# The first part of the query weights as two loads of 64 partitions from two queues, in a decode kernel of attention and a mixing MLP

## The chip, the cores and the metric

The kernel runs on one core of a Trainium2 chip. The core has five engines with queues of their own: TensorE (PE, matrix products), VectorE (DVE), ScalarE (ACT), GpSimd (POOL) and SyncE (SP), and 16 DMA engines that move data between the chip's main memory and the core's SBUF of 128 partitions. In this kernel loads are issued by SyncE and, for one small one, by ScalarE. The metric is the device time of one execution in microseconds (us); lower is better.

## What is computed

One token passes through two layers. The first is attention with a cache of keys and values: 32 query heads, 8 key heads, 16,384 cached positions of 128 values each; the second is a layer norm, a small mixing block and an MLP of width 1792. With one token, the mixing block's shifts by one or two positions leave nothing but zeros, so only x itself passes through it.

```python
def _A_ref(x, k_cache, v_cache, wq, wo):
    q = (x @ wq).reshape(B, Sq, Hq, Dh).transpose(0, 2, 1, 3)
    k = jnp.repeat(k_cache, rep, axis=1)
    v = jnp.repeat(v_cache, rep, axis=1)
    scores = jnp.einsum("bhqd,bhkd->bhqk", q, k) * (Dh ** -0.5)
    p = _softmax(scores, axis=-1)
    o = jnp.einsum("bhqk,bhkd->bhqd", p, v)
    return o.transpose(0, 2, 1, 3).reshape(B, Sq, Hq * Dh) @ wo

h = x + _A_ref(_layernorm(x), k_cache, v_cache, wq, wo)
x1 = hn + hs        # hn = _layernorm(h); hs is zero for one token
return h + x1 + _gelu(_layernorm(x1) @ w3) @ w4
```

Everything is bf16. The two caches are 33.6 MB each, wq and wo 4.2 MB each, w3 and w4 1.8 MB each: 79.2 MB are read once.

## The kernel before

The 8 key heads are worked through in four pairs. For each pair 8.4 MB of keys go to the buffer kb (two halves of 128 x 32 KB) and 8.4 MB of values to vb (128 partitions of 64 KB). VectorE transposes the keys into kt (line 656), TensorE multiplies them with the query (line 667), a softmax follows on VectorE and ScalarE, and TensorE multiplies its result with the values (line 708). The buffer vb first holds the query weights wq (4 rows of wq, 32 KB, in each partition), and kb at the end holds wo, w3 and w4.

The program is written as a list of operations for each engine, with the tiles that each reads and writes; from these a small class derives the waits. Within an engine the order is the order of writing. All large loads are issued by SyncE through the helper load (line 474, the line that the profile shows for every load), in this order: the query weights in two loads, the keys of pair 0, the values of pair 0, and so on to wo, w3 and w4. A load waits only until its buffer has been read for the last time.

At the start (lines 586 to 590) ScalarE issues the load of x (1 KB, as 4 rows of 128 values), and SyncE the first WQ = 2048 columns of each partition's share of wq ("wq0", 4 KB a partition, 0.5 MB), then the other 28 KB a partition ("wq1", 3.5 MB), then the first keys. Meanwhile GpSimd makes an identity matrix and clears two tiles (lines 608 and 609), VectorE copies a corner of the identity to the tile quarter (line 601, which waits for x), TensorE spreads x over the partitions with it (line 603), and VectorE works out the layer norm's mean and root (lines 544 to 582) and some masks (lines 611 to 620). The tile xn (line 623) is the normed x. It waits for both weight loads, and the 32 products of line 632 that make the query wait for it. When these are done vb is free and SyncE issues the first values.

Of the kernel before, what the change touches and what calls it, by code (L numbers as in the profile page):

```python
# [356 lines left out]
NCH = D // 128  # L357
# [3 lines left out]
WQ = 2048  # L361
WO = ((0, 20), (20, 32))
VP = 1
# [22 lines left out]
def bass_sequential_preLN__gqa_block_cached__mixer_s_mlp__decode_kernel(  # L386
# [13 lines left out]
    with ExitStack() as ctx:  # L400
# [26 lines left out]
        st = [sb(f"st{i}", [128, 16], FP32) for i in range(2)]  # L427
        added = sb("added", [128, 2], FP32)
        sti = [sb(f"sti{i}", [128, 2, 2], I32) for i in range(2)]
        xn = sb("xn", [128, NCH], BF16)  # L430
# [23 lines left out]
        hT = sb("hT", [128, NCH, 32], FP32)  # L454
# [6 lines left out]
        wq_sb, wo_sb = vb, kb[0]  # L461
# [11 lines left out]
        def load(name, dst, src, key, by="SP", also=()):  # L473
            P.op(by, lambda e: e.dma_start(dst, src), w=[key, *also], dma=name)  # L474
# [54 lines left out]
        def piece(cuts, m):  # L529
            return [lo <= m < hi for lo, hi in cuts].index(True)  # L530
# [52 lines left out]
                r=[(S, 8), (T, 0)], w=[(S, 6 + n) for n in ns])  # L583


        load("x4", x4[:, :], A_x[0, 0:1, :].rearrange("o (q j) -> (o q) j", q=4), "x4", "ACT")
        wq_in = A_wq.rearrange("(p k) c -> p (k c)", k=NCH)
        load("wq0", wq_sb[:, 0:WQ], wq_in[:, 0:WQ], "wq0")
        load("wq1", wq_sb[:, WQ:NCH * HQ * DH], wq_in[:, WQ:NCH * HQ * DH], ("v", 0), also=[("v", x) for x in range(1, VP)])
        load_keys(0, 0)  # L590

# [1 line left out]
        for n in range(2):  # L593
# [8 lines left out]
            r=["ident_f", "x4"], w=["quarter"])  # L602
# [9 lines left out]
            r=["ident_f"], w=["row32"])  # L612
        dve(lambda e: e.tensor_reduce(maskdd[:, :], ident_f[:, :].rearrange("p (n d) -> p d n", d=4), AX.X, ALU.add),
            r=["ident_f"], w=["maskdd"])
# [3 lines left out]
        for z, src, key, of, n in ((zo, row32[:, :].rearrange("p (g n h) -> p g h n", g=2, h=REP), "zo", "row32", 4),  # L618
# [3 lines left out]
                src.unsqueeze(3).to_broadcast([128, 2, REP, 4, n]), AX.X, ALU.add), r=[of], w=[key])  # L622
        dve(lambda e: e.tensor_scalar(xn[:, :], hT[:, :, 0], st[0][:, 0:1], st[0][:, 6:7],  # L623
                                      ALU.add, ALU.mult),
            r=["hT", (("st", 0), 0), (("st", 0), 6), "wq0"] + [("v", x) for x in range(VP)], w=["xn"])

        keys = [("s", 0), ("s", 1), ("O", 0), ("O", 1), "A", "mn", "spare0", "spare1"]
        wq_k = wq_sb[:, 0:NCH * HQ * DH].rearrange("p (k c) -> p k c", k=NCH)
        for i, key in enumerate(keys):
            P.part("query", i)  # L630
            for k in range(NCH):
                pe(lambda e, k=k: e.matmul(row[:, bass.ds(P.b + P.b0, 512)], copies(xn[:, k:k + 1], 128),  # L632
                                           wq_k[:, k, bass.ds(P.c + P.c0, REP * DH)], start=(k == 0), stop=(k == NCH - 1)),
                   r=["xn"], also=[("v", x) for x in range(VP)], w=["n" if key == "mn" else key], bank=[key])
        P.part()
        for g in range(2):
            half = banks[64 * g:64 * g + 64, PAIRS * g:PAIRS * g + PAIRS, :].rearrange("p j c -> p (j c)")
            for b in range(2):
# [3 lines left out]
                    r=["n" if x == "mn" else x for x in keys[PAIRS * g:PAIRS * g + PAIRS]], w=["qcol"],  # L642
# [141 lines left out]
        for n, (lo, hi) in enumerate(W4):  # L784
# [4 lines left out]
            r=["o_m"], w=["o_f"])  # L789
        dve(lambda e: e.tensor_copy(o_b[:, :], o_f[:, :]), r=["o_f", ("r", 0, 0)], w=["o_b"])  # L790

        for r_ in range(32):
# [4 lines left out]
               r=["o_b"] + [("r", 0, n) for n in (piece(WO, r_),) if n], w=[("O", 0)], bank=[("O", 0)],  # L797
# [4 lines left out]
        for n in range(2):  # L802
            dve(lambda e, n=n: e.tensor_copy(osum[:, 256 * n:256 * n + 256], O_ps[0][:, 256 * n:256 * n + 256]),  # L803
                r=[("O", 0)], w=[("osum", n)], bank=[("O", 0)])
        for q in range(4):
            pe(lambda e, q=q: e.matmul(h_ps[32 * q:32 * q + 32, 0:128], copies(row32[:, 0:1], 32),
                                       osum[:, q * 128:(q + 1) * 128], start=True, stop=True),
               r=[("osum", q // 2), "row32"], w=[hkey], bank=[hkey])
# [4 lines left out]
            r=["hT", (S, 0)] + [("r", 1, 0)], w=["hc"])  # L813
# [3 lines left out]
        for k in range(NCH):  # L817
            for q in range(4):
                pe(lambda e, k=k, q=q: e.matmul(s_ps[32 * q:32 * q + 32, 0, 0:FQ], hc[:, k, :],
                                                w3_sb[:, k, q * FQ:(q + 1) * FQ], start=(k == 0), stop=(k == NCH - 1)),  # L820
                   r=["hc"] + [("r", 1, n) for n in (piece(W3, k),) if n], w=[("s", 0)], bank=[("s", 0)])
# [4 lines left out]
            r=["xs", (S, 6), "hr"], w=[hkey], bank=[hkey])  # L826
# [9 lines left out]
        for m in range(NHC):  # L836
# [5 lines left out]
            for o in range(4):  # L842
# [5 lines left out]
                   r=[("hcol", 2 * m // NHC)] + [("r", 1, len(W3) + n) for n in (piece(W4, m),) if n],  # L848
                   w=[hkey], bank=[hkey])
# [7 lines left out]
             r=[("fin", 0), ("fin", 1)], w=["out"], dma="out")  # L857
# [32 lines left out]
```

## Time and profile before

| | |
|---|---|
| runs timed, median (lowest to highest) | 189.47 us (189.44 to 189.67), 3 runs |
| profiled execution: span from the first to the last instruction | 188.3 us |
| mean clock granted to TensorE in it | 0.916 |
| busy: PE, DVE, ACT, POOL | 124.1, 115.8, 13.7, 4.6 us |
| read from main memory | 79.17 MB, 420 GB/s over the span |
| first issue of a load | 0.73 us |
| last load (w4) lands | 186.2 us |

The page gives the profiled execution's span and no other time of it. Its times count from the span's start. "L656" is line 656 of the kernel, "kt<-kb" is an operation that reads kb and writes kt, and "<-DMA" after a time says that a transfer ended the engine's wait. A name with q (SPq, ACTq) is an engine's instruction queue, where a load is issued; the transfer itself runs on the DMA engines behind it. q1 is the DMA queue of SyncE's loads, q10 that of ScalarE's.

### The profile page before, as it was taken

How to read it: one execution, taken by the hardware profiler on the slowest of the kernel's cores; microseconds unless marked ns; L12 is line 12 of the kernel's file. 1: busy time of each engine (PE TensorE's matmuls, PEld its weight loads, DVE VectorE, ACT ScalarE, POOL GpSimd, SP SyncE). 2: the span in 40 equal slices, each digit the busy share in tenths (PEclk: the TensorE clock that was granted, in tenths of full speed). 3: DMA queues.
4: the chain of work that ended last, by engine and by line, in shares of the span. 5: the costliest groups of instructions: out<-in, count | busy, mean ns of one | idle time of the engine just before them, and what ended most of it. 6: DMA issues, size and time to landing. Idle time of an engine off the chain costs nothing.

```text
span 188.3 us, 2375 instructions
## 1 busy us (share of the span) xinstructions
PE 124.1 (66%) x760; PEld 48.3 (26%) x761; DVE 115.8 (62%) x138; ACT 13.7 (7%) x21; POOL 4.6 (2%) x8
## 2 busy tenths in 40 slices
PE   0109700698979978897910019799799889775772
PEld 0104200233322522332500003333244333222221
DVE  5730741999636998936300069993699898633173
ACT  3000200000004000004000000000400000500012
POOL 8100000000000000000000000000000000000000
PEclk9999985569999999999995557999999999999999
DMA  7999999999799999987999999998999996999994
GB/s 252 445 418 445 445 445 446 445 445 445 334 445 446 445 557 418 418 390 334 446 445 445 445 446 445 445 445 334 445 446 445 543 390 292 445 432 411 433 429 193
DMA packets 2607, 79.19 MB, mean 421 GB/s; under 512 B 302, under 2 KB 430, under 8 KB 686
## 3 DMA queue, kind: packets, MB, share of 16 engines
q1 hardware_dynamic: 2598, 79.17, 98.0%
q8 instruction: 1, 0.02, 0.0%
q10 hardware_dynamic: 8, 0.00, 0.0%
HBM read 79.17 MB, written 0.00 MB: 420 GB/s over the span
## 4 chain that ended last, share of the span: by engine, by line
DMA 69%; DVE 23%; PE 4%; issue 3%; SPq 1%; DVEq 0%
DMA kb<-in_A_k_cache_dram 54%; DVE kt L656 22%; DMA kb<-in_B_w_dram 15%; PE banks L667 3%; SPq L474 1%; PE banks L845 0%; DVE fin L852 0%; DVEq L147 0%; DVE den L725 0%; PE banks L524 0%; DVE od L723 0%; SPq L147 0%
## 5 line engine op out<-in xcount | busy, mean ns | idle before, releaser
L667 PE MATMUL banks<-kt,qn 128*128 x256 | 68.1, 401 | 36.8 <-DVE kt L656 35.7
L656 DVE STREAM_TRANSPOSE kt<-kb 128x2048 int32<-128x2048 int32 (+2 forms) x24 | 70.6, 2994 | 27.5 <-DMA kb<-in_A_k_cache_dram 26.4
L667 PEld LDWEIGHTS banks<-kt,qn 128*128 x256 | 25.4, 100 | 79.4 <-issue 65.5
L518 PE MATMUL banks<-qb 128*128 128x512 bf16 x61 | 22.1, 387 | 0.7 <-issue 0.2
L708 PE MATMUL banks<-vb,pt 128*32 128x512 bf16 x256 | 14.7, 379 | 1.1 <-POOLq L500 1.1
L693 ACT ACTIVATE p_sb<-banks,bias 128x1024 bf16<-128x1024 f32 x4 | 4.5, 1114 | 133.3 <-DVE nmh L688 133.3
L632 PE MATMUL banks<-vb,xn 128*128 x32 | 8.5, 432 | 6.7 <-DVE xn L623 6.7
L697 DVE STREAM_TRANSPOSE pt<-p_sb 64x1024 bf16<-64x1024 bf16 x8 | 9.9, 1239 | 4.4 <-ACT p_sb L693 4.3
L681 DVE TENSOR_REDUCE mx<-banks 128x1 f32<-128x1024 f32 x4 | 4.9, 1224 | 10.5 <-PE banks L667 10.5
L518 PEld LDWEIGHTS banks<-qb 128*128 128x128 bf16 x62 | 5.9, 97 | 16.0 <-issue 15.7
L708 PEld LDWEIGHTS banks<-vb,pt 128*32 128x32 bf16 x256 | 8.5, 97 | 5.4 <-POOLq L500 1.2
L639 DVE STREAM_TRANSPOSE qcol<-banks 64x1024 f32<-64x1024 f32 x4 | 4.8, 1227 | 6.7 <-PE banks L632 6.7
L632 PEld LDWEIGHTS banks<-vb,xn 128*128 128x128 bf16 x32 | 3.5, 108 | 11.4 <-issue 8.7
L676 ACT ACTIVATE banks<-mean 128x1024 f32<-128x1024 f32 x4 | 4.1, 1027 | 18.6 <-DVE qcol L639 18.5
L684 PE MATMUL banks<-mxd,mean 128*128 128x128 f32 x8 | 2.0, 326 | 4.7 <-DVE mxd L682 4.7
L732 DVE SCALAR_TENSOR_TENSOR od<-banks,rowc,od 128x128 f32<-128x128 f32 x12 | 4.2, 350 | 0.4
L794 PE MATMUL banks<-kb,o_b 128*32 128x512 bf16 x44 | 3.3, 384 | 1.6 <-DVE o_b L790 1.1
L729 DVE TENSOR_SCALAR od<-banks,rowc 128x128 f32<-128x128 f32 x4 | 1.3, 319 | 4.6 <-PE banks L708 4.6
L603 PE MATMUL banks<-x,quarter 4*128 4x128 bf16 x1 | 0.3, 286 | 5.4 <-DVE quarter L601 5.4
L601 DVE CAST quarter<-ident_f 4x128 bf16<-4x128 f32 x1 | 2.9, 2901 | 1.3 <-DMA x<-in_A_x_dram 1.3
L737 PE MATMUL banks<-od,zo 128*32 128x128 f32 x10 | 2.0, 283 | 1.8 <-DVE od L732 1.6
L803 DVE COPY osum<-banks 128x256 f32<-128x256 f32 x2 | 0.8, 418 | 4.0 <-PE banks L794 4.0
(74 smaller groups left out, 39.5 us busy)
## 6 DMA issues: line engine op xcount, KB each, us to landing
kb<-in_A_k_cache_dram SPq DMA_DIRECT2D x4, 4096.0 KB, 20.5
vb<-in_A_wq_dram SPq DMA_DIRECT2D x1, 3584.0 KB, 11.7
kb<-in_A_wo_dram SPq DMA_DIRECT2D x1, 2560.0 KB, 26.2
kb<-in_B_w_dram SPq DMA_DIRECT2D x1, 1792.0 KB, 24.4
kb<-in_A_wo_dram SPq DMA_DIRECT2D x1, 1536.0 KB, 29.5
kb<-in_B_w_dram SPq DMA_DIRECT2D x1, 1024.0 KB, 26.6
kb<-in_B_w_dram SPq DMA_DIRECT2D x1, 640.0 KB, 27.7
vb<-in_A_wq_dram SPq DMA_DIRECT2D x1, 512.0 KB, 3.6
```

The costliest lines, as they stand in the source:

```text
L518: P.op("PE", lambda e: e.matmul(O_ps[1][:, :], field[:, 0:128], field[:, 0:512], start=True, stop=True), r=["qb"], bank=[("O", 1)], times= ...
L632: pe(lambda e, k=k: e.matmul(row[:, bass.ds(P.b + P.b0, 512)], copies(xn[:, k:k + 1], 128), wq_k[:, k, bass.ds(P.c + P.c0, REP * DH)], sta ...
L639: dve(lambda e, g=g, b=b, half=half: e.transpose(qcol[64 * g:64 * g + 64, 2 * b:2 * b + 2, :, :].rearrange("p e m u -> p (e m u)"), half.r ...
L656: P.op("DVE", lambda e, t=t, n=n: e.transpose(pieces(kt, t, n).bitcast(I32), pieces(kb[y], t, n).bitcast(I32)), r=[("r", y, i) for i in ra ...
L667: pe(lambda e, n=n: e.matmul(row[:, bass.ds(P.y, 512)], qn[:, n, bass.ds(P.q, 128)], key_piece(P.k, n), start=False, stop=(n == 3), skip_g ...
L676: act(lambda e: e.activation(s_all, copies(mean4[:, 0:1], 1024), ACTF.Identity, scale=0.0), r=["mean4", "p"], w=[("s", 0), ("s", 1)], **both)
L681: dve(lambda e: e.tensor_reduce(mx[:, :], s_all, AX.X, ALU.max), r=[("s", 0), ("s", 1)], w=["mx"], **both)
L693: act(lambda e: e.activation(p_sb[:, :], s_all, ACTF.Exp, bias=bias[:, 0:1], scale=float(SCALE), accum_out=acc[:, :]), r=[("s", 0), ("s", ...
L697: dve(lambda e, g=g: e.transpose(pt[64 * g:64 * g + 64, :, :, g, :], p_sb[64 * g:64 * g + 64, :]), r=["p"], w=["pt"])
L708: pe(lambda e, l=l, ct=ct, ch=ch: e.matmul(O_ps[0][32 * ct:32 * ct + 32, :], pt[:, l, ch, :, :].rearrange("p g u -> p (g u)"), tiles[:, l ...
L732: dve(lambda e, block=block, c=c: e.scalar_tensor_tensor(od[:, :], block, rowc[:, c:c + 1], od[:, :], ALU.mult, ALU.add), r=[key, "rowc", ...
L794: pe(lambda e, r_=r_, q=q: e.matmul(O_ps[0][32 * q:32 * q + 32, :], copies(o_b[:, r_:r_ + 1], 32), wo_sb[:, r_ * D:(r_ + 1) * D], start=(r ...
```

## The change

The first weight load is cut by partitions: SyncE loads 4 KB of each of partitions 0 to 63, and ScalarE the same of partitions 64 to 127. The load of x is written behind ScalarE's half. xn waits for both halves and, as before, for the second weight load. Each half has a semaphore of its own.

```diff
+        wq_in = A_wq.rearrange("(p k) c -> p (k c)", k=NCH)
+        for g, by in enumerate(("SP", "ACT")):
+            load(f"wq{by}", wq_sb[64 * g:64 * g + 64, 0:WQ], wq_in[64 * g:64 * g + 64, 0:WQ], ("wq0", g), by)
         load("x4", x4[:, :], A_x[0, 0:1, :].rearrange("o (q j) -> (o q) j", q=4), "x4", "ACT")
-        wq_in = A_wq.rearrange("(p k) c -> p (k c)", k=NCH)
-        load("wq0", wq_sb[:, 0:WQ], wq_in[:, 0:WQ], "wq0")
         load("wq1", wq_sb[:, WQ:NCH * HQ * DH], wq_in[:, WQ:NCH * HQ * DH], ("v", 0), also=[("v", x) for x in range(1, VP)])
         load_keys(0, 0)
...
         dve(lambda e: e.tensor_scalar(xn[:, :], hT[:, :, 0], st[0][:, 0:1], st[0][:, 6:7],
                                       ALU.add, ALU.mult),
-            r=["hT", (("st", 0), 0), (("st", 0), 6), "wq0"] + [("v", x) for x in range(VP)], w=["xn"])
+            r=["hT", (("st", 0), 0), (("st", 0), 6), ("wq0", 0), ("wq0", 1)] + [("v", x) for x in range(VP)], w=["xn"])
```

On SyncE, at the program's start, there stood before (vb is the buffer of the query weights and the values, kb that of the keys; shapes are partitions x elements of 2 bytes; in brackets the semaphores waited for):

```order
0 L474 DMA vb<-in_A_wq_dram 128x2048 [waits barrier_Pool_Activation_PE_DVE_SP_release]
1 L474 DMA vb<-in_A_wq_dram 128x14336
2 L474 DMA kb<-in_A_k_cache_dram 128x32768
3 L474 DMA vb<-in_A_v_cache_dram 128x32768 [waits e_PE,e_DVE,d_wq1]
4 L474 DMA kb<-in_A_k_cache_dram 128x16384 [waits e_DVE,d_k0]
```

and now:

```order
0 L474 DMA vb<-in_A_wq_dram 64x2048 [waits barrier_Pool_Activation_PE_DVE_SP_release]
1 L474 DMA vb<-in_A_wq_dram 128x14336
2 L474 DMA kb<-in_A_k_cache_dram 128x32768
3 L474 DMA vb<-in_A_v_cache_dram 128x32768 [waits e_PE,e_DVE,d_wq1]
4 L474 DMA kb<-in_A_k_cache_dram 128x16384 [waits e_DVE,d_k0]
```

The first load has half the partitions; nothing else of SyncE's queue has moved. On ScalarE, at the program's start, there stood before (scr and banks are a scratch tile and the result banks of TensorE; L607 is there for its table alone):

```order
0 L474 DMA x<-in_A_x_dram 4x128 [waits barrier_Pool_Activation_PE_DVE_SP_release]
1 L607 ACT_TABLE_LOAD
2 L607 ACTIVATE scr<-mean 1x1 [waits e_DVE]
3 L676 ACTIVATE banks<-mean 128x1024 [waits e_PE,e_DVE]
4 L693 ACTIVATE p_sb,acc<-banks,bias 128x1024 [waits e_DVE,e_PE]
5 L676 ACTIVATE banks<-mean 128x1024 [waits e_ACT]
```

and now, with the line numbers behind the loads one higher:

```order
0 L474 DMA vb<-in_A_wq_dram 64x2048 [waits barrier_Pool_Activation_PE_DVE_SP_release]
1 L474 DMA x<-in_A_x_dram 4x128
2 L608 ACT_TABLE_LOAD
3 L608 ACTIVATE scr<-mean 1x1 [waits e_DVE]
4 L677 ACTIVATE banks<-mean 128x1024 [waits e_PE,e_DVE]
5 L694 ACTIVATE p_sb,acc<-banks,bias 128x1024 [waits e_DVE,e_PE]
```

The weight load stands where x's load stood, and x's load, the table load and the first activation are one place later. TensorE's, VectorE's and GpSimd's instructions stand in the same order as before.

## The prediction

> **What bounds the kernel now.** I read the page's chain and DMA rows first, then the chain in order of time, then SyncE's own issues, and last the first 5 us in small slices. First the page of before: span, busy share of the 16 DMA engines in 40 slices, GB/s, the queue, the chain.
>
> ```profile
> span 188.3 us, 2375 instructions
> DMA  7999999999799999987999999998999996999994
> GB/s 252 445 418 445 445 445 446 445 445 445 334 445 446 445 557 418 418 390 334 446 445 445 445 446 445 445 445 334 445 446 445 543 390 292 445 432 411 433 429 193
> q1 hardware_dynamic: 2598, 79.17, 98.0%
> DMA 69%; DVE 23%; PE 4%; issue 3%; SPq 1%; DVEq 0%
> ```
>
> The queue that SyncE feeds (q1) keeps 16 engines busy for 98% of the span; no compute engine comes near. Single slices dip (334 beside 557) because a packet is counted as a whole where it falls. The next row is the view of stages: from 12.05 to 186 us the DMA share is 1.00, at 431 GB/s.
>
> ```profile
> 12.05:186.00 173.95, 122.62 (x733) 47.32 (x734) 108.02 (x113) 11.96 (x18) 0.00 (x0) 0.91 1.00 431
> ```
>
> The chain names VectorE for 23%, so I ask whether VectorE ever leaves the queue empty. The chain in order of time (start, us, what), cut to the places where the stream is handed on:
>
> ```profile
> 0.73 0.40 SPq L474
> 1.18 0.42 SPq L474
> 1.65 30.58 DMA kb<-in_A_k_cache_dram
> ...
> 50.18 20.82 DMA kb<-in_A_k_cache_dram
> ...
> 127.47 20.37 DMA kb<-in_A_k_cache_dram
> ...
> 158.53 27.68 DMA kb<-in_B_w_dram
> 186.22 0.04 issue
> ```
>
> and SyncE's issues of the value loads and of the output weights:
>
> ```profile
> 22.39 0.33 SPq L474 DMA_DIRECT2D vb<-in_A_v_cache_dram  x1
> 65.56 0.33 SPq L474 DMA_DIRECT2D vb<-in_A_v_cache_dram  x1
> 142.67 0.33 SPq L474 DMA_DIRECT2D vb<-in_A_v_cache_dram  x1
> 147.92 0.80 SPq L474 DMA_DIRECT2D kb<-in_A_wo_dram  x2
> ```
>
> Each load is issued before the one ahead of it has landed: the first values at 22.39 while the first keys land at 32.23 (1.65 + 30.58), 9.8 us ahead; the second at 65.56 against 71.00, 5.4 us ahead; the last at 142.67 against 147.84, 5.2 us ahead. So the kernel is one stream of 79.17 MB, begun by the first load of the query weights and ended by w4 at 186.22, with a tail of about 2 us. **A shift of this stream at its start is a shift of the end**, as long as it is under 5 us. The change touches only its start.
>
> The start, from the DMA view of the first 5 us in 40 slices of 0.125 us (busy share, then GB/s):
>
> ```profile
> DMA  0000000000000099469894879999999990009999
> GB/s 0 0 0 0 0 0 0 0 0 0 0 0 0 4 229 164 135 131 164 164 328 164 262 328 426 459 590 786 918 1114 590 459 459 0 0 0 688 1147 459 459
> ```
>
> SyncE issues at 0.73 and bytes move from 1.75. The eleven slices from 1.75 to 3.125 add up to 2495, times 0.125 us: 0.312 MB in 1.375 us, 227 GB/s, which at 431 would take 0.72 us. So **the ramp costs 0.65 us** of the stream, and the engines are mostly busy in it: it is slow packets rather than missing ones. From about 3.1 us on the rate is full.
>
> **The change, part by part.**
>
> *The split.* The first 4 KB of each of 128 partitions, 0.524 MB, is now two loads of 0.262 MB. Bytes, and packets of 4 KB, stay as they are; 0.524 MB at 431 GB/s is 1.22 us either way. What an issue costs, from the instructions of the loading line:
>
> ```profile
> L474 SPq DMA_DIRECT2D vb<-in_A_v_cache_dram x4: 328/328/328, 22.4 to 142.7; - x4
> L474 SPq DMA_DIRECT2D vb<-in_A_wq_dram x2: 398/410/421, 0.7 to 1.2; - x2
> L474 ACTq DMA_DIRECT2D x<-in_A_x_dram x1: 546/546/546, 0.7 to 0.7; - x1
> 187.14 0.32 SPq L855 DMA_DIRECT2D out_dram<-fin  x1
> ```
>
> An issue of 8 MB takes 328 ns, one of 1 KB 0.32 us: it does not depend on the size. So halving the first load makes SyncE's issue no shorter than 0.32 instead of 0.40 (gain at most 0.08 us); and the next load, issued by 1.60, is not needed until the rate is full at about 3.1, so an earlier issue of it buys nothing. On the other side, ScalarE's issue of 1 KB took 546 ns when it began at 0.73 together with SyncE's of 398 to 421: two issues at once make one of them some 0.15 us later (546 less 398). That is now the issue of half the bytes. While SyncE's half is moving it may lie hidden; at worst it is 0.15 us. I take **+0.1**, nearer to the ScalarE row, since that is the queue which now carries it. Bounds: -0.08 and +0.15.
>
> *One more load's completion.* x's queue had 8 packets for its 4 rows, so a load has small packets of its own beside its data. Their time in the first 5 us:
>
> ```profile
> q10 hardware_dynamic: 8, 0.00, 0.1%
> ```
>
> 0.1% of 16 x 5 us is 0.08 us for 8, so 0.01 us each: one more on every engine is nothing.
>
> *How fast two half loads move.* The trace has no load of 64 partitions, and no two large loads from two queues at once, so this is bounded. Below: if the second queue filled all the ramp, -0.65 us. Above: at full rate 128 partitions take 431 GB/s; if the limit lies with the partitions, 64 take 215, and if the halves then moved one after the other, 0.524 MB would take 2.44 us instead of 1.22: +1.22. I take **0**, the nearest row being the first 5 us themselves: there x's queue and SyncE's already ran side by side, and the ramp was there all the same. Both ends stay for the range.
>
> *x behind ScalarE's half.* The timeline's rows of x's issue, of the work that waits for it, and of what that work stands beside:
>
> ```profile
> 0.73 0.55 ACTq L474 DMA_DIRECT2D x<-in_A_x_dram  x1
> 2.49 2.90 DVE L601 CAST quarter<-ident_f 4x128 bf16<-4x128 f32 x1 [1.32 <-DMA x<-in_A_x_dram]
> 3.51 1.80 POOL L609 MEMSET pt<- 128x2048 bf16 x1
> 9.88 1.04 DVE L620 TENSOR_REDUCE zd<-ident_f 128x32 f32<-128x512 f32 x1
> 12.99 0.29 DVE L623 TENSOR_SCALAR xn<-hT,st 128x4 bf16<-128x4 f32 x1 [2.06 <-DMA vb<-in_A_wq_dram]
> 21.27 1.03 ACT L676 ACTIVATE banks<-mean 128x1024 f32<-128x1024 f32 x1 [18.47 <-DVE qcol L639]
> 25.64 0.32 DVE L754 COPY qn<-qb 128x624 bf16<-128x624 bf16 x1
> 32.33 8.83 DVE L656 STREAM_TRANSPOSE kt<-kb 128x2048 int32<-128x2048 int32 x3 [6.36 <-DMA kb<-in_A_k_cache_dram]
> ```
>
> x's issue moves from 0.73 to behind another ScalarE issue of about 0.55, and its 1 KB stands behind 0.262 MB. The cast ended at 5.39 and the chain behind it at 10.92, so from the end of the cast 5.5 us are needed; xn then waits 2.06 us for the second load of weights. If x came at 5.4, the cast (it ended just as GpSimd's memset did, at 5.31) would still let xn start on time. If x came as late as the weights, at 12.9, xn would begin at about 18.5, 5.5 us late, and with it the issue of the values (22.39 to 27.9, still before 32.23) and the last step before the keys (25.96 to 31.5, still before 32.33). So **x costs 0** at either end; its cover is the landing of the first keys, and if that were gone it would cost its delay past 2.06 us. The table load and the first activation of ScalarE move behind with it; ScalarE's next work, the clearing of the score banks, is at 21.27. The two semaphores that xn now waits for instead of one are those of loads that landed long before the weights it waits for anyway.
>
> **Sum.** Against the span: 188.3 + 0.1 + 0 + 0 = 188.4 us. The page gives no time of that execution other than its span; the median of the runs, 189.47, lies 1.17 us above it, and I keep that difference: 189.57, **189.6 us**.
>
> **Rivals.** *A, slower: the halves take turns.* If 64 partitions take at most 215 GB/s, SyncE's half, whose bytes come first, holds all 16 engines at that rate, and ScalarE's half after it does too. In the ramp that costs little, since 227 GB/s is all that moved there. What moved at full rate, 0.524 - 0.312 = 0.212 MB, takes 0.99 us instead of 0.49: +0.5; without the ramp's cover +1.2. It decides the sign against my forecast as soon as over 0.2 MB move at half rate. Price +0.6: 190.1. For it: all bytes of a queue's half go to one half of the partitions, and nothing in the program makes the two halves keep step. Against it: no row shows a limit by partitions, and two halves that alternate on each engine would share out evenly.
>
> The Trainium skill, "SBUF — State Buffer", section "Door 1: The DMA port swizzle", says that partitions 0 to 63 reach only half of the ports by which DMA enters, and that such a load runs at about the rate of 32 partitions; its section on issuing two DMAs for the two halves found them only 6% faster than one. "DMA: Bandwidth & Descriptors", section "Rules for kernel authors", advises one load of 128 partitions for that reason. By these the sum would be rival A's upper end; no run so far shows it.
>
> *B, faster: the second queue fills the ramp.* The ramp is slow packets; if a second queue lets each engine have another packet under way while the first is waited for, up to 0.65 us come back. Price -0.5: 189.0. For it: the busy share in the ramp falls to 4 and 6 tenths in places. Against it: a single queue had all of its packets issued by 1.13, and still got 131 to 164 GB/s around 2.1 us.
>
> *C, x late beyond its cover:* needs x later than any load ahead of it; 189.6 plus what exceeds 9 us. Hardly possible.
>
> **How the numbers follow.** A measurement of this kernel can tell about 0.2%, 0.38 us, from no change: 189.09 to 189.85. Forecast 0.54, A 0.33, B 0.12, C 0.01. Faster is B, same is the forecast and C, slower is A. The range goes from 189.0 (B's price) to 190.4 (between A's price and its end at 190.7), which leaves out some 0.15; the forecast alone would have 189.3 to 189.8.
>
> **What would show it.** The two weight loads among the DMA issues (KB, us from issue to landing):
>
> ```profile
> vb<-in_A_wq_dram SPq DMA_DIRECT2D x1, 3584.0 KB, 11.7
> vb<-in_A_wq_dram SPq DMA_DIRECT2D x1, 512.0 KB, 3.6
> ```
>
> The landing of the second (1.18 + 11.7 = 12.9) and of the first keys at 32.23 move by the same amount as the end: by 0.1 if I am right, by half a microsecond or more later under A, earlier under B. The slices from 1.75 to 3.6 us show where: a plateau near 215 GB/s after 3 us is A, a rate above 300 before 2.5 us is B. The cast should start later than 2.49 and xn still wait for the weights. I am wrong if the end moves while the first keys land when they did, or if SyncE's first bytes come later than 1.75.

## The result, and the profile after

The changed kernel took 190.64 us in the median of 6 runs (190.44 to 190.74), the kernel before 189.57 in 6 runs beside it: **1.07 us slower**, a ratio of 1.0056 with a 95% interval from 1.0044 to 1.0067. The forecast was 189.6, the range ended at 190.4: the time lies above it, on the side of rival A.

First the page of after: the same lines as before the prediction, and now a row for ScalarE's queue, q10.

```profile
span 189.3 us, 2377 instructions
DMA  7999999999799999999999999997999989999994
GB/s 202 394 512 443 443 443 443 443 429 429 312 408 422 443 436 443 443 443 443 443 443 443 443 443 443 443 443 332 443 443 436 492 388 402 402 424 426 435 407 181
q1 hardware_dynamic: 2534, 78.91, 97.2%
q10 hardware_dynamic: 88, 0.26, 0.5%
DMA 69%; DVE 23%; PE 4%; issue 3%; SPq 1%; DVEq 0%
```

It is the same stream: same chain, same rate in the middle. Only the first slices are poorer: 202 and 394 GB/s where there were 252 and 445. The chain in order of time says where the time came in:

```profile
0.73 0.55 SPq L474
1.34 0.57 SPq L474
1.96 31.52 DMA kb<-in_A_k_cache_dram
...
51.29 20.96 DMA kb<-in_A_k_cache_dram
...
128.95 20.07 DMA kb<-in_A_k_cache_dram
...
159.70 27.56 DMA kb<-in_B_w_dram
187.26 0.04 issue
```

The first keys land at 33.48 (1.96 + 31.52) instead of 32.23, 1.25 us later; the last load at 187.26 instead of 186.22, 1.04 us later. The loss is complete within the first 33 us and all but 0.2 us of it is carried to the end. The first 5 us in slices of 0.125 us:

```profile
DMA  0000000000000000741897896977979499989906
GB/s 0 0 0 0 0 0 0 0 0 0 0 0 0 0 0 0 98 98 66 164 328 229 164 262 229 229 229 295 459 229 590 131 754 524 885 262 721 688 0 229
```

and the issues of the loading line (least, median and greatest ns):

```profile
L474 SPq DMA_DIRECT2D vb<-in_A_wq_dram x2: 548/559/570, 0.7 to 1.3; - x2
L474 ACTq DMA_DIRECT2D vb<-in_A_wq_dram x1: 550/550/550, 0.7 to 0.7; - x1
```

Two things differ. Bytes move from the slice at 2.0 us instead of 1.75 (the first 4 KB packet begins at 2.08 instead of 1.76), behind issues of 0.55 instead of 0.40 us. And from 2.5 to 3.5 us the rate stays between 164 and 328 GB/s, where it had climbed past 400 at 3 us. x came late, but cost nothing:

```profile
8.56 0.21 DVE L602 CAST quarter<-ident_f 4x128 bf16<-4x128 f32 x1 [7.38 <-DMA x<-in_A_x_dram]
14.26 0.29 DVE L624 TENSOR_SCALAR xn<-hT,st 128x4 bf16<-128x4 f32 x1
24.86 0.33 SPq L474 DMA_DIRECT2D vb<-in_A_v_cache_dram  x1
33.58 2.31 DVE L657 STREAM_TRANSPOSE kt<-kb 128x2048 int32<-128x2048 int32 x1 [5.14 <-DMA kb<-in_A_k_cache_dram]
```

The cast waits for x until 8.56 instead of 2.49, xn starts 1.27 us later than before and waits for nothing at its own turn, and the values are issued at 24.86, still 8.6 us ahead of the first keys.

### The profile page after: what moved, and what is told of

It reads as the page before. It is cut to its first block, busy times and chain, and to the rows that moved or that the text cites. A ratio compares the mean times of both kernels' runs of the same rounds, so it can differ in the third digit from the quotient of the medians.

```text
span 189.3 us, 2377 instructions
## 1 busy us (share of the span) xinstructions
PE 127.2 (67%) x761; PEld 49.2 (26%) x761; DVE 113.1 (60%) x138; ACT 13.7 (7%) x21; POOL 4.6 (2%) x8
## 4 chain that ended last, share of the span: by engine, by line
DMA 69%; DVE 23%; PE 4%; issue 3%; SPq 1%; DVEq 0%
DMA kb<-in_A_k_cache_dram 54%; DVE kt L657 23%; DMA kb<-in_B_w_dram 15%; PE banks L668 3%; SPq L474 1%; PE banks L846 0%; DVE fin L853 0%; DVEq L147 0%; DVE den L726 0%; PE banks L524 0%; DVE od L724 0%
## 5 line engine op out<-in xcount | busy, mean ns | idle before, releaser
L633 PE MATMUL banks<-vb,xn 128*128 x32 | 9.7, 478 | 4.6 <-DVE xn L624 4.6
L795 PE MATMUL banks<-kb,o_b 128*32 128x512 bf16 x44 | 4.6, 542 | 1.1 <-DVE o_b L791 1.1
L602 DVE CAST quarter<-ident_f 4x128 bf16<-4x128 f32 x1 | 0.2, 214 | 7.4 <-DMA x<-in_A_x_dram 7.4
## 6 DMA issues: line engine op xcount, KB each, us to landing
vb<-in_A_wq_dram SPq DMA_DIRECT2D x1, 3584.0 KB, 12.8
```

What stands on the lines that cost most here:

```text
L795: pe(lambda e, r_=r_, q=q: e.matmul(O_ps[0][32 * q:32 * q + 32, :], copies(o_b[:, r_:r_ + 1], 32), wo_sb[:, r_ * D:(r_ + 1) * D], start=(r ...
```

## The experiments

Two theories stood against each other. P: a load of 64 partitions moves at half rate (rival A). Q: two large loads that are issued at once by two queues hold each other up. Times are medians, each beside further runs of the kernel before (189.41, 189.52, 189.46 or 189.55 us), and ratios are to these, with 95% intervals. The diffs show the loads alone; where a load is new, the list of what xn waits for names it too. Packet times are those of the single DMA packets in the run's trace.

**The halves on one queue.** The changed kernel with both halves issued by SyncE and x alone on ScalarE:

```diff
-        for g, by in enumerate(("SP", "ACT")):
+        for g, by in enumerate(("SP", "SP")):
...
```

> Both halves of 64 partitions are issued by SyncE, one after the other; x alone on ScalarE as before. After the change the second weight load landed 1.25 us later than before (1.34 + 12.8 against 1.18 + 11.7, less than 0.1 of it lost again by the end) and the first 4 KB packets began about 0.3 us later. Theory P (a load of 64 partitions moves at half the rate): most of the loss stays, +0.6 to +1.2 us against the kernel before. Theory Q (two large loads issued at once by two queues delay each other): the loss is gone, within 0.2 us of the kernel before. Both at work: about +0.7, and the first bytes move from 1.75 as before.

191.48 us, ratio 1.0102 (1.0067 to 1.0137): 2.1 us by the medians, more than either theory had. Taking the second queue away did not take the loss away. But the six runs lie from 190.28 to 192.71, far apart for this kernel; the experiment mixes in something of its own, which is taken up below.

**Columns instead of partitions, on two queues.**

```diff
-  load(f"wq{by}", wq_sb[64 * g:64 * g + 64, 0:WQ], wq_in[64 * g:64 * g + 64, 0:WQ], ("wq0", g), by)
+  load(f"wq{by}", wq_sb[:, g * WQ // 2:(g + 1) * WQ // 2], wq_in[:, g * WQ // 2:(g + 1) * WQ // 2], ("wq0", g), by)
```

> Two queues as in the change, x behind ScalarE's load, but the cut is by columns: each queue loads 2 KB of all 128 partitions. P: no loss beyond the smaller packets, within 0.2 us of the kernel before. Q: nearly the whole loss, +0.8 to +1.2. Both at work: +0.3 to +0.5, with both issues at about 0.55 us instead of 0.40 and the first bytes at about 2.0 to 2.1.

189.44 us, ratio 1.0001 (0.9991 to 1.0011): no loss at all. Its issues:

```profile
L474 SPq DMA_DIRECT2D vb<-in_A_wq_dram x2: 398/418/437, 0.7 to 1.2; - x2
L474 ACTq DMA_DIRECT2D vb<-in_A_wq_dram x1: 390/390/390, 0.7 to 0.7; - x1
```

and its first 5 us in slices:

```profile
GB/s 0 0 0 0 0 0 0 0 0 0 0 0 0 0 82 164 262 131 164 164 229 311 328 410 377 426 573 442 1377 1729 705 0 0 0 0 0 459 1376 1376 459
```

Two queues issue at the same time, each in 0.39 to 0.40 us, bytes move from 1.75, and 400 GB/s are reached before 3 us. **Q falls.** It also shows that the longer issue comes with the loads of 64 partitions and not with a second queue. It does not stay with them: in the change the second weight load, all 128 partitions of it, was issued behind SyncE's half in 0.57 us (1.34 in the chain above), where it had taken 0.42 before.

**The suspected cost seven times as large.** The kernel before, with the second weight load (3.67 MB) cut into partitions 0 to 63 and 64 to 127, both issued by SyncE:

```diff
-  load("wq1", wq_sb[:, WQ:NCH * HQ * DH], wq_in[:, WQ:NCH * HQ * DH], ("v", 0), also=[("v", x) for x in range(1, VP)])
+  for g in range(2):
+      load(f"wq1{g}", wq_sb[64 * g:64 * g + 64, WQ:NCH * HQ * DH], wq_in[64 * g:64 * g + 64, WQ:NCH * HQ * DH], ("v", 0) if g else ("wq1", 0))
```

> The kernel before, but the second weight load (28 KB of each partition, 3.67 MB) is issued by SyncE as two loads of 64 partitions: the suspected cost made seven times as large. P: 3.67 MB at half of 431 GB/s take 17.0 us instead of 8.5, so the first keys land some 8 us later and the end is later by 8 us. Q: within 0.3 us of the kernel before, since nothing is issued by a second queue.

198.81 us, ratio 1.0488 (1.0463 to 1.0512): 9.4 us. The view of stages has it plainly (the last column is GB/s, the one before it the DMA share): while the halves load, and afterwards.

```profile
5.00:20.00 15.00, 0.87 (x3) 0.60 (x3) 4.83 (x21) 0.00 (x0) 0.32 (x1) 1.00 1.03 214
21.00:60.00 39.00, 25.02 (x83) 9.32 (x83) 23.98 (x16) 1.03 (x1) 0.00 (x0) 0.82 0.98 422
```

The engines are just as busy, at half the rate. A busy share cannot tell that; the GB/s can, and so can the packets of 28 KB, which took 2.24 us in the median instead of 1.06.

**The same on two queues**, the upper half issued by ScalarE behind x:

```diff
...
-  ("v", 0) if g else ("wq1", 0))
+  ("v", 0) if g else ("wq1", 0), "ACT" if g else "SP")
```

> The kernel before, but the second weight load (28 KB of each partition) cut into partitions 0 to 63 by SyncE and 64 to 127 by ScalarE behind x. On one queue this cut cost 9.4 us, with packets of 2.24 us. If the halves take turns whatever queues carry them: about +8 to +9. If packets of two queues alternate on each engine and the halves share out: under +2, with packets near 1.06 us, and then the loss in the changed kernel comes from ScalarE's half being late.

197.93 us, ratio 1.0446 (1.0424 to 1.0468): 8.4 us. In the stage:

```profile
5.00:19.00 14.00, 0.87 (x3) 0.60 (x3) 4.83 (x21) 0.00 (x0) 0.31 (x1) 1.00 1.02 225
```

Two queues do not let the halves share out: 225 against 214 GB/s. The packets of this trace do alternate between the queues on each engine, but nearly in step: in each turn from 4.9 to 16 us, 13 of the 16 engines were on one half and three on the other, and a packet took 2.0 to 2.2 us on either. Why the three were no faster, the trace does not show.

**Which partitions, or how many.** The kernel before, with the second weight load as partitions 32 to 95, then 0 to 31, then 96 to 127:

```diff
-  load("wq1", wq_sb[:, WQ:NCH * HQ * DH], wq_in[:, WQ:NCH * HQ * DH], ("v", 0), also=[("v", x) for x in range(1, VP)])
+  for g, (lo, hi) in enumerate(((32, 96), (0, 32), (96, 128))):
+      load(f"wq1{g}", wq_sb[lo:hi, WQ:NCH * HQ * DH], wq_in[lo:hi, WQ:NCH * HQ * DH], ("wq1", g) if g < 2 else ("v", 0))
```

> The kernel before, but the second weight load is issued by SyncE as partitions 32 to 95, then 0 to 31, then 96 to 127. Theory W (the limit is which partitions: those below 64 share one half of the way into SBUF, those above the other): the middle load has both and moves at full rate, packets of 1.06 us; the two outer ones of 32 partitions move at half rate, 0.92 MB in 4.3 us instead of 2.1 each, so +4 to +5 us. Theory N (each partition takes at most 3.4 GB/s, so the count decides): the middle load's packets take 2.24 us as in the halves, and the outer ones move at a quarter of the full rate: 8.5 + 8.5 + 8.5 instead of 8.5 us, +17 us.

193.88 us, ratio 1.0233 (1.0215 to 1.0250): 4.4 us, as W had it. The middle load, the outer two, and what follows:

```profile
4.50:7.60 3.10, 0.87 (x3) 0.60 (x3) 2.25 (x9) 0.00 (x0) 0.82 (x1) 1.00 1.03 435
9.30:15.50 6.20, 0.00 (x0) 0.00 (x0) 1.62 (x5) 0.00 (x0) 0.00 (x0) 1.00 1.05 222
16.00:60.00 44.00, 28.78 (x98) 10.68 (x98) 25.08 (x17) 1.03 (x1) 0.00 (x0) 0.84 0.99 424
```

Sixty-four partitions move at 435 GB/s when they lie on both sides of 64, and 32 on one side at 222. **It is which partitions, not how many.** The packets of the middle load took 1.06 us, the full rate, those of the outer two 1.7 at first and then 2.0 to 2.2 (medians of 16).

The Trainium skill has a reason for it in "SBUF — State Buffer", section "Door 1: The DMA port swizzle": partitions below 64 reach one half of the ports by which DMA enters and those above the other, with about 218 GB/s for a half. The 214 and 222 here agree. Its section on issuing two DMAs for both halves has two of them 6% faster than one. The nearest rows here, two queues against one, are 225 and 214 GB/s, 5%.

**How much is the start.** The changed kernel with SyncE loading the even partitions and ScalarE the odd ones, so that each load of 64 lies on both sides:

```diff
...
-  wq_sb[64 * g:64 * g + 64, 0:WQ], wq_in[64 * g:64 * g + 64, 0:WQ]
+  wq_sb[g:128:2, 0:WQ], wq_in[g:128:2, 0:WQ]
```

> The changed kernel, but SyncE loads the even partitions and ScalarE the odd ones: two loads of 64 partitions as in the change, each with 32 below 64 and 32 above. Theory W (the halves of the partitions share one way in each): what is left of the loss of 1.07 us is what a load of 64 partitions costs to begin, an issue of 0.55 us instead of 0.40 and first bytes 0.33 us later: +0.3 to +0.5. If any load of 64 partitions moves slowly unless its 16 engines reach different partitions groups, packets stay above 0.2 us and the loss stays near +1.

189.97 us against 189.46, ratio 1.0034 (1.0021 to 1.0048): 0.5 us by the medians, 0.4 to 0.9 by the interval. Issues and first bytes are those of the change:

```profile
L474 SPq DMA_DIRECT2D vb<-in_A_wq_dram x2: 544/558/573, 0.7 to 1.3; - x2
L474 ACTq DMA_DIRECT2D vb<-in_A_wq_dram x1: 545/545/545, 0.7 to 0.7; - x1
```

```profile
GB/s 0 0 0 0 0 0 0 0 0 0 0 0 0 0 0 0 98 229 295 295 197 360 262 229 197 197 393 459 295 426 1311 328 2065 0 229 0 0 0 231 229
```

The ramp behind them is over sooner than in the change (1311 in the slice from 3.75 and 2065 in that from 4.0, against 590 and 754). The packets show the rate itself: ScalarE's 64 packets of 4 KB took 0.25 us in the median in the change, 0.16 here, and 0.16 was the median of all the 4 KB packets in the kernel before. SyncE's 64, which lie in the ramp, took 0.16 in the change as well. So about half of the loss goes with the start of a load of 64 partitions, wherever they lie; the rest, 0.2 to 0.7 us by the same interval, is what the cut at 64 adds, the rate. The one execution that was profiled was the fastest of the eight (189.62), and in it the first keys landed only 0.2 us late (1.96 + 30.48 = 32.44), so the start's share is not sharper than its interval.

**How much is the rate.** The halves with 8 KB of each partition, and the kernel before with the same 8 KB as its control:

```diff
-WQ = 2048
+WQ = 4096
```

> The changed kernel with 8 KB of each partition instead of 4 KB in the two halves (1.05 MB), to be compared with the kernel before with the same 8 KB. If the loss is the halves' rate, it grows by 0.524 MB at half of 431 GB/s against 431: by 1.2 us, to 2.2 or 2.3 us. If it is a late start alone, it stays at 1.0 to 1.1. The part that does not grow is the start's: 1.07 less what 0.524 MB adds.

> The kernel before with 8 KB of each partition in the first load of query weights and 24 KB in the second; the control of the run above. Both theories: within 0.2 us of the kernel before.

191.80 us, ratio 1.0122 (1.0107 to 1.0136), against 189.37 for the control, ratio 1.0000 (0.9988 to 1.0011). The loss went from 1.07 us to 2.31 (0.0122 x 189.46): **the second 0.524 MB cost 1.24 us, against 1.22 by half the rate.** The intervals of the two losses (0.8 to 1.3 and 2.0 to 2.6 us) leave about 0.35 us either way, so that the agreement to 0.02 is luck. A late start alone, which would have left the loss where it was, is excluded. The first 0.524 MB cannot have cost that much beside the start's half microsecond; some of it lay in the ramp, where the rate is no higher than half anyway.

**x ahead of ScalarE's half** in the changed kernel:

```diff
+  load("x4", x4[:, :], A_x[0, 0:1, :].rearrange("o (q j) -> (o q) j", q=4), "x4", "ACT")
   for g, by in enumerate(("SP", "ACT")):
...
-  load("x4", x4[:, :], A_x[0, 0:1, :].rearrange("o (q j) -> (o q) j", q=4), "x4", "ACT")
```

> The changed kernel, with x's load ahead of ScalarE's half instead of behind it. Q: SyncE's half begins as the first load did before, at about 1.75, since it meets only x's issue; the loss falls to +0.3 or less. P: the halves still move at half rate, and ScalarE's comes 0.55 us later: +0.7 to +1.2. If x's place behind the half had any part in the loss, this run is the faster one of the two by that part.

190.89 us, ratio 1.0076 (1.0054 to 1.0099): the loss stays, and at 1.0 to 1.9 us it is if anything larger, with ScalarE's half issued at 1.33 instead of 0.74. SyncE's issue of 64 partitions takes 0.55 us beside x's small one too, and the first 4 KB packet begins at 2.06. x's place behind the half had no part in the loss.

**x on SyncE**, between the two weight loads of the kernel before, tried as a gain:

```diff
-  load("x4", x4[:, :], A_x[0, 0:1, :].rearrange("o (q j) -> (o q) j", q=4), "x4", "ACT")
   load("wq0", wq_sb[:, 0:WQ], wq_in[:, 0:WQ], "wq0")
+  load("x4", x4[:, :], A_x[0, 0:1, :].rearrange("o (q j) -> (o q) j", q=4), "x4", "SP")
```

> The kernel before, with x's load issued by SyncE between the two weight loads, so that ScalarE issues no load at all. If x's issue beside SyncE's first one holds up the first bytes (1.75 us, about 1.0 us after the issue, where the output's 1 KB needed some 0.75), the stream starts up to 0.3 us earlier and the end with it: -0.1 to -0.3 us. If two queues at once cost nothing, as the column halves on two queues suggest: within 0.1 us of the kernel before; x lands near 4.4 instead of 2.4 and the cast still ends before xn needs it.

189.83 us, ratio 1.0023 (1.0001 to 1.0044). Bytes still moved from 1.75: x's issue was not what they waited for. No gain, and again the spread: eight of the twelve runs lie from 189.28 to 189.96, four from 190.86 to 191.05. The trace is of one of the four (190.86). In its packets one of the 16 DMA engines begins the first keys at 13.88 us, the others from 12.08 to 12.73, and about the same distance is there when w4 ends, the last packet at 187.17 us and the other engines' by 186.03: one engine was late from the start, and late to the end.

**Column halves on one queue.**

```diff
-        for g, by in enumerate(("SP", "ACT")):
+        for g, by in enumerate(("SP", "SP")):
...
```

(on the kernel with the column halves)

> The column halves again (2 KB of all 128 partitions twice), both issued by SyncE. If the two queues neither gain nor lose anything: within 0.2 us of the kernel before, like the column halves on two queues. If there a gain of the second queue covered a loss by packets of 2 KB: slower than that run by the gain, 0.2 to 0.6 us.

192.14 us, ratio 1.0133 (1.0115 to 1.0152). Neither had it: 2.5 us, with no load under 128 partitions. What this has in common with the halves on one queue and with x on SyncE is that the large load of 28 KB a partition is issued third. The trace cannot size it, since it is of the fastest of the five runs, 190.23, only 0.7 us above the kernel before. Even there the first 28 KB packets of the 16 engines took 1.06 to 2.05 us, 1.45 in the median, where the kernel before has 1.06 to 1.19, and the first keys begin from 12.29 to 13.40 instead of 12.09 to 12.51. That gave the last experiment, on the kernel before: as many loads, the large one second.

```diff
-  load("wq0", wq_sb[:, 0:WQ], wq_in[:, 0:WQ], "wq0")
+  load("wqh0", wq_sb[:, 0:WQ // 2], wq_in[:, 0:WQ // 2], ("wq0", 0))
   load("wq1", wq_sb[:, WQ:NCH * HQ * DH], wq_in[:, WQ:NCH * HQ * DH], ("v", 0), also=[("v", x) for x in range(1, VP)])
+  load("wqh1", wq_sb[:, WQ // 2:WQ], wq_in[:, WQ // 2:WQ], ("wq0", 1))
```

> The column halves on one queue cost 2.5 us, though no load had fewer than 128 partitions; there the large second load was issued third, at 1.7 us instead of 1.2. Here SyncE issues 2 KB of all partitions, then the large load of 28 KB, then the other 2 KB, then the first keys: as many loads, but the large one is second again. If the loss came from the large load being issued third and some engine running out of packets before it came: within 0.2 us of the kernel before. If it comes from four loads in a row on one queue: +1 to +2.5 us again.

189.76 us against 189.55, ratio 1.0008 (0.9996 to 1.0019). Four loads in a row are harmless if the large one is the second. The first keys begin from 12.20 to 12.57 us in its trace, though the first 28 KB packets took 1.08 to 1.66, so slow first packets alone are not the cost. The halves on one queue issue it third. In that run's trace (191.70), too, one engine begins the first keys at 14.83 us, the others from 13.01 to 13.82, and its last packet of w4 ends at 188.12, the others' by 187.20. So that run held this cost beside that of its partitions and cannot be used to size either.

No version beat the kernel before: the column halves on two queues and 8 KB in the first load are its equals.

## Why the prediction was wrong

What bounds the kernel was read rightly: one stream, whose start is carried to the end. The loss appears at 33 us and stays. x cost nothing, by the cover that was named, though it came at 8.56, later than the 5.4 up to which no step would move.

**The step that failed is "How fast two half loads move: I take 0."** The trace of before had no load of 64 partitions, and the nearest row, x's queue beside SyncE's, said nothing of one. In its place the runs showed the mechanism of rival A, half the rate for a load on one side of 64, and about its price: after the start's share of 0.4 to 0.9 us, 0.2 to 0.7 us are left for the rate, around the "+0.5" that was worked out from 0.212 MB beyond the ramp. The signs that were named for A came too: 229, 229 and 229 GB/s in the slices from 3.0 us, and the second weight load landing 1.26 us later (1.34 + 12.8). Both arguments against A fell. "No row shows a limit by partitions" was true and no evidence, since nothing in the kernel could have shown one. That two halves which alternate on each engine would share out evenly was tested with the large load: they did alternate, and lost 8.4 us on two queues, against 9.4 on one.

**The second step that failed is the cost of the split's issue.** From an issue of 8 MB at 328 ns and one of 1 KB at 0.32 us it followed that size does not matter. A load of half the partitions still took longer: SyncE's half took 0.55 us to issue where the whole load had taken 0.40, the load behind it 0.57 instead of 0.42, and bytes moved 0.25 to 0.33 us later, which the prediction had named as a sign of being wrong. The term was bounded from -0.08 to +0.15; the even and odd halves measured about +0.5 (0.4 to 0.9). The row that was read as "two issues at once" was that of x (4 partitions, 546 ns); beside SyncE's issue, a load of 128 partitions from ScalarE took 390. With +0.5 in the place of +0.1, rival A would have come to 189.47 + 0.5 + 0.5 = 190.5, above the range; its loss of 1.0 us is close to the 1.07 measured, but neither part is known that well.

Rival B had nothing: the column halves put two queues to work on the ramp at no loss, and it stayed about as slow, 238 GB/s from 1.75 to 3.125 us against 227.

## What to carry to other kernels

Cut a load by columns, not by partitions: two loads of 64 partitions on either side of 64 move at half rate, on one queue or two, and a busy DMA share hides it. If a cut by partitions is needed, let each load lie on both sides of 64 (32 to 95 moved at full rate). At the head of a stream, issue the large load early: a second small load ahead of it cost up to 2.5 us here, and behind it nothing that could be measured. In the two slow executions of that kind that were traced, one engine was late at the first keys and still late at the end; why it was late is not shown.

## What the runs showed that was not expected

- The issue of a load of 64 partitions took 0.51 to 0.58 us, of one of 128 partitions at the head of the program 0.35 to 0.44, whether the bytes are 4, 8 or 28 KB a partition and whichever partitions they are. But a load of 128 partitions just behind one of 64 took 0.57 to 0.59 too, and x behind ScalarE's half 1.00 where it took 0.58 behind ScalarE's 128 partitions. Why, no run here tells, nor how much of the start's half microsecond it is.
- One more small load ahead of the large one on the same queue cost 2.5 us (column halves) and spread the runs over 2 us; with the large one second it cost at most 0.4. What holds the large load's packets back on some engines was not tried further.
- Seven times the bytes in halves cost 9.4 us, not the 8.5 of a rate cut to half. The packets of 28 KB took 2.24 us, somewhat over twice 1.06, and the first 64 KB packets of the keys behind them 2.6 to 3.1 us instead of 2.42. Why is open.
